# Batch 1's q loaded ahead of two weight tiles, and the last two o quarters of chunk 0 with jt outermost, in an attention and Swish-FFN kernel

## The chip, the core and the metric

The kernel runs on one core of a Trainium2 chip. The metric is device time in microseconds, from one launch to its end. A program's instructions run on five engines, each with its own queue: TensorE (PE, with its weight loads shown apart as PEld), VectorE (DVE), ScalarE (ACT), GpSimd (POOL) and SyncE (SP), which here only issues DMAs. Instructions of one engine run in the order of the program; between engines, semaphores order them.

## What is computed

Eight batches of 8 heads, 576 positions (S), 64 features (D). First a linear attention with a cosine weighting, then a feed-forward layer whose gate is a sigmoid with its own beta per feature:

```python
c, s = cos(pi/2 * pos / S), sin(pi/2 * pos / S)
phi(x) = concat([relu(x) * c, relu(x) * s])      # 64 -> 128 features
kv  = phi(k).T @ v ;  z = sum(phi(k))            # per batch and head
num = phi(q) @ kv  ;  den = phi(q) @ z + 1e-6
x   = (num / den)                                # 4608 tokens x 512
h   = x @ w_in                                   # 512 -> 2048
g   = h * sigmoid(beta * h)
out = g @ w_out                                  # 2048 -> 512
```

Inputs and output are float32; the matmuls run in bf16 with float32 sums.

## The kernel before

**Tiling.** The 4608 tokens are cut into 9 chunks (c) of 512. A chunk has 32 slots. Slots 0 to 15 are `h_group` (L376): for each of 16 blocks of 128 hidden features (jt), four matmuls of 128x512 (`h_mm`, L366) and one Silu on ACT (`h_act`, L373), which makes the tile g. Slots 16 to 31 are the second layer, `o_mm` (L387): four token tiles (tt) of 128 rows, each the sum over the 16 jt, cut into four parts of four jt. In chunk 0 the order is part outermost: slots 16 to 27 walk tt within a part (`o_part`), and slots 28 to 31 each do two tt and two jt (L593). When a tile's last jt is done, ACT copies the sum out (L399) and POOL issues two stores (L386).

**Attention in between.** 64 tokens of one batch's eight heads come from 9 groups (n). For a batch: `q_relu` and `k_relu` (DVE, L190), `v_scale` (DVE L215 and ACT L213), `kv_mm` (PE, L260, 72 small matmuls), `kv_take` out of PSUM (ACT L270 or DVE L272), a turn (transpose) of q, `num_mm` (PE, L281), the division `x_rden` and `x_mul` (DVE, L292 to L303) and a turn of the result into xt, which h_mm reads. From batch 2 on the turns are DMA transposes, and `att_units` puts the batch's work between the slots of the chunk before. For batches 0 and 1 the turns run on PE: `q_turn_pe` (L222), whose two parts are copied out by its `take` (ACT to qt, L235; DVE times tan to qs, L218), and `x_turn_pe` (L335). Chunk 1's tokens are the last group of batch 0 and seven groups of batch 1, so batch 1 has to be ready at the end of chunk 0.

**What sets the order.** The schedule is written by hand: the order of the calls is the order on each engine. The dictionary `early` (L537) says what is done after which slot of chunk 0. Batch 1's sums (`kv_mm`) come after slot 22, its two turns of q after 25 and 26, `num_seven` after 28 and 29, the turns of xs inside slots 30 and 31, around a part of chunk 1's first h matmuls.

**PSUM** is one tile of 8 banks, which the code hands out by number: `h_bank` (L357) for h, and for o of chunk 0 banks 2, 3, 0, 1 for tt 0 to 3.

**Weights and loads.** w_in and w_out come in as float32, four tiles each, through four stage buffers, and are cast to bf16: w_in by DVE and POOL (`cast_win`, L98), w_out by DVE or ACT with a factor 1/beta (`cast_wout`, L110). A stage of w_out can only be loaded when the casts of the w_in tile in the same buffer are done. The loads are issued by SP, in the order of `rest()` (L510): w_out 0 and 1, batch 1's v and k, w_out 2, batch 1's q, w_out 3; batch 2's q, v, k come after slot 24. raw_q, raw_v and raw_k have two buffers each.

**Warm-up matmuls.** `warm_pe` (L418) multiplies zeros, to keep PE busy in the first 20 us: among others 4 of 128 columns (L448), 2 of 512 (L476) and 1 of 512 ahead of the first h matmul (L495).

Of the kernel before, what the change touches and what calls it, by code (L numbers as in the profile page):

```python
# [12 lines left out]
AF = mybir.ActivationFunctionType  # L13
ALU = mybir.AluOpType
# [3 lines left out]
NQ = 9  # L18
# [4 lines left out]
def kernel(  # L23
# [14 lines left out]
    nc = tc.nc  # L38
# [49 lines left out]
    def load_w(kind, i, step=4):  # L88
        if (kind, i) not in stages:
            stages[kind, i] = stage.tile([P, 4, 512], FP32, name="w_stage", tag="w_stage")  # L90
        st = stages[kind, i]
        if kind == "out":
            nc.sync.dma_start(out=st, in_=w_out_v[:, 4 * i : 4 * i + 4, :])
            return
        for a in range(0, 4, step):
            nc.sync.dma_start(out=st[:, a : a + step], in_=w_in_v[:, a : a + step, i * 512 : (i + 1) * 512])

    def cast_win(i, gj, eng="dve", f0=0, f1=512, jps=slice(0, 2)):  # L98
# [8 lines left out]
        else:  # L107
            nc.vector.tensor_copy(o, a)  # L108

    def cast_wout(i, engs="dddd"):  # L110
        st = stages["out", i]
        for jj in range(4):
            j = 4 * i + jj
            if engs[jj] == "a":
                nc.scalar.activation(wout[i][:, jj, :], st[:, jj, :], AF.Copy, scale=rbeta[:, j : j + 1])
            else:
                nc.vector.tensor_scalar(wout[i][:, jj, :], st[:, jj, :],
                                        scalar1=rbeta[:, j : j + 1], scalar2=None, op0=ALU.mult)

    GJ = [(0, 0), (0, 1), (1, 0), (1, 1)]  # L120

# [70 lines left out]
    def q_relu(b, jp, eng="dve"):  # L192
        relu(qb[:, jp].rearrange("q n (j d) -> q j n d", j=2), raw_tile(b, "q")[:, 2 * jp : 2 * jp + 2], eng)
# [28 lines left out]
    def q_turn_pe(b, jp, bank, hold=False):  # L222

        parts = ((0, 0, 5), (1, 5, NQ))
        v2 = []
        for i, n0, n1 in parts:
            t = ps[:, bank + i].bitcast(BF16)[:, 0 : (n1 - n0) * P].rearrange("q (n c) -> q n c", c=P)
            v2.append(t)
            for n in range(n0, n1):
                nc.tensor.matmul(t[:, n - n0, :], lhsT=qb[:, jp, n, :], rhs=ident,  # L230
                                 is_transpose=True, start=(n == n0), stop=(n == n1 - 1))
        def take(e, i):
            _, n0, n1 = parts[i]
            if e == "act":
                nc.scalar.copy(qt[:, jp, n0:n1], v2[i])  # L235
            else:
                tan_mul(nc.vector, qs[:, jp, n0:n1], v2[i], n0, n1)

        if hold:
            return take  # L240
        for e, i in (("act", 0), ("dve", 1), ("act", 1), ("dve", 0)):
            take(e, i)
# [11 lines left out]
    def kv_mm(b, jp, bank, jjs=(0, 1)):  # L254
        t = kv_out(jp, bank)
        for n in range(NQ):
            for jj in jjs:
                for g in range(2):
                    hs = slice(g * HP, (g + 1) * HP)
                    nc.tensor.matmul(  # L260
                        t[jj * HP : (jj + 1) * HP, g], lhsT=rk[hs, n, 2 * jp + jj, :],
                        rhs=vb[hs, n, 2 * jp + jj].rearrange("q s e -> q (s e)"),
                        start=(n == 0), stop=(n == NQ - 1))

    def kv_take(jps, bank, eng="dve"):
        a0, a1 = jps[0], jps[-1] + 1
        o = kv[:, :, a0:a1].rearrange("q g s c e -> q g (s c e)")
        a = ps[:, bank : bank + 2, a0 * 2 * E : a1 * 2 * E]
        if eng == "act":
            nc.scalar.copy(o, a)  # L270
        else:
            nc.vector.tensor_copy(o, a)  # L272
# [83 lines left out]

    def h_bank(c, jt):  # L357
        if c < 2 and jt < 4:
            return ((3, 2, 0, 1), (6, 7, 2, 3))[c][jt]
        return ((6, 7, 4, 5) if c == 0 else (4, 5, 0, 1))[jt % 4]  # L360

    def h_mm(c, jt, mis=range(4), blocks=slice(0, NB)):
        xt = xt_tile(c)
# [7 lines left out]
    def h_act(c, jt):  # L371
        g_t = gt_pool.tile([P, TCH], BF16, name="g_t", tag="g_t")
        nc.scalar.activation(g_t, ps[:, h_bank(c, jt)], AF.Silu, scale=beta[:, jt : jt + 1])  # L373
        gs[c, jt] = g_t
# [10 lines left out]
            eng = (nc.sync, nc.scalar)[hf] if two else nc.sync if c >= 7 else nc.gpsimd  # L385
            eng.dma_start(out=out_v[bb, n][:, m0:m1], in_=o_sb[hf * HP : (hf + 1) * HP, m0:m1])  # L386

    def o_mm(c, tt, jts, between=None):
        o_ps = ps[:, (2, 3, 0, 1)[tt] if c == 0 else 2 + tt % 2]
        for jt in jts:  # L390
            nc.tensor.matmul(o_ps, lhsT=gs[c, jt][:, tt * P : (tt + 1) * P],  # L391
                             rhs=wout[jt // 4][:, jt % 4, :],
                             start=(jt == 0), stop=(jt == JT - 1))
        if jts[-1] < JT - 1:
            return
        if between:
            between()
        o_sb = osb_pool.tile([P, DM], FP32, name="o_sb", tag="o_sb")
        nc.scalar.copy(o_sb, o_ps)  # L399
        store(c, tt, o_sb)  # L400
# [17 lines left out]
    def warm_pe(count, w=512, bank=1):  # L418
        for i in range(count):
            nc.tensor.matmul(ps[:, bank, 0:w], lhsT=zeros[:, 0:P], rhs=zeros[:, 0:w], start=True, stop=True)  # L420
# [24 lines left out]
    warm_pe(8, 128, bank=0 + 2)  # L445
    q_turn_pe(0, 0, 4)
    nc.vector.reciprocal(rbeta, beta)
    warm_pe(4, 128)  # L448
    take = q_turn_pe(0, 1, 2, hold=True)
    warm_long(4)  # L450
    take("act", 0)
# [21 lines left out]
    got = x_rden(2, 0, 0, 7, (0,))  # L473
    got2 = x_rden(4, 0, 7, 8, (0,))
    k_relu(0, 3, 4, "dve", 0, 5)
    warm_pe(2, bank=1)  # L476
    kv_mm(0, 1, 6)
    x_mul_act(got2, 7)
    kv_take((1,), 6, eng="act")
# [12 lines left out]
    x_mul(got, 0, 4)  # L492
    x_mul(got, 4, 7)
    x_mul(x_rden(6, 0, 7, 8, (1,)), 7, 8)
    warm_pe(1, bank=3)  # L495
    h_mm(0, 0, (0, 1))
    h_mm(0, 1, (0, 1))
    x_turn_pe(0, 0, 4, 4, ("act",), (1,))
# [11 lines left out]
    def rest():  # L510

        cast_halves(2, (0,))
        x_mul(x_rden(2, 0, 8, NQ, (0, 1)), 8, NQ)
        cast_halves(2, (256,))
        cast_halves(3)
        load_w("out", 0)
        load_w("out", 1)
        load_raw(1, "v")
        load_raw(1, "k")
        load_w("out", 2)  # L520
        load_raw(1, "q")
        load_w("out", 3)
        cast_wout(0)
        cast_wout(1)
        v_scale(1, 0)
        k_relu(1)
        cast_wout(2)
        q_relu(1, 0)


    def num_seven(jp, bank):
        for n in range(7):
            num_mm(n, jp, bank, n)

    takes = []
    turns = (("act", 0), ("dve", 1), ("act", 1), ("dve", 0))
    early = {  # L537
        4: lambda: (num_mm(8, 0, 2, 0), num_mm(8, 1, 2, 1), rest()),
        9: lambda: x_turn_pe(0, 8, 9, 3),
        15: lambda: v_scale(1, 1, eng="act"),  # L540
        22: lambda: (kv_mm(1, 0, 6), kv_mm(1, 1, 6), kv_take((0, 1), 6, "act"), q_relu(1, 1)),
        25: lambda: takes.append(q_turn_pe(1, 0, 4, hold=True)),
        26: lambda: (takes.append(q_turn_pe(1, 1, 6, hold=True)),
                     [takes[0](*t) for t in turns], cast_wout(3, "adda"),
                     [takes[1](*t) for t in turns]),
        28: lambda: (num_seven(0, 4), x_mul(x_rden(4, 0, 0, 7, (0,)), 0, 7)),
        29: lambda: (num_seven(1, 6), x_mul(x_rden(6, 0, 0, 7, (1,)), 0, 7)),
        31: lambda: ([h_mm(1, jt, (0, 1)) for jt in range(2)], x_turn_pe(1, 0, 7, 5, ("dve",), (1,)),
                     [h_mm(1, jt, (0, 1)) for jt in range(2, 4)]),
    }  # L550

    def num_rest():
        for n in range(7, NQ):
            for jp in range(2):
                num_mm(n, jp, 0, 2 * (n - 7) + jp)
        x_mul(x_rden(0, 0, 7, NQ, (0, 1)), 7, NQ)
        x_turn_dma(1, 7, NQ)

    def att_units(b):
# [21 lines left out]
    for slot in range(32):  # L581
        if slot < 4:
            if slot == 0:
                for jt in range(4):
                    h_mm(0, jt, (2, 3), slice(0, 4))
            h_mm(0, slot, (2, 3), slice(4, 8))
            h_act(0, slot)
        elif slot < 16:
            h_group(0, slot)
        elif slot < 28:  # L590
            o_part(0, slot % 4, (slot - 16) // 4)
        else:
            for tt in (2 * (slot % 2), 2 * (slot % 2) + 1):  # L593
                o_mm(0, tt, range(12, 14) if slot < 30 else range(14, 16),
                     (lambda: x_turn_pe(1, 0, 7, 4, ("act",), (0,))) if tt == 0 else None)
        if slot == 24:
            for name in "qvk":
                load_raw(2, name)
        if slot in early:
            early[slot]()  # L600
    for c in range(1, NTC):
        units = att_units(c + 1) if c + 1 < B else []
        for slot in range(32):
            if c == 1 and slot < 4:
                h_mm(c, slot, (2, 3))
                h_act(c, slot)
            elif slot < 16:
                h_group(c, slot)
            elif c == NTC - 1 and slot >= 28:
                if slot == 28:  # L610
                    o_last(c, 3)
            else:
                o_part(c, (slot - 16) // 4, slot % 4)
            while units and units[0][0] <= slot:
                units.pop(0)[1]()
# [30 lines left out]
```

## Time and profile before

| | |
|---|---|
| median of 4 runs | 295.53 us (295.15 to 296.5) |
| the profiled execution's own time | 296.5 us |
| its span, from first to last instruction | 294.7 us |
| granted TensorE clock, mean | 0.994 |
| PE busy | 287.0 us, 97% of the span |
| HBM read / written | 36.71 MB / 9.44 MB |

The profile is of one execution, the slowest of the four. Times in it count from the start of the span; the 1.8 us between span and time lie outside it. Rows of a timeline give the start, the length and the engine, the line in the code, the operation, what is written and read, and how many instructions were merged; in brackets how long the engine stood idle before, and what ended that. A PE row's length goes to the modelled end of its last matmul, so rows overlap: the distance between the starts of two rows is what the first took. An issue on SP lasts as long as the queue keeps it waiting for space; the time at which the data lands is in the DMA view.

### The profile page before, as it was taken

Reading aid. Unit: us, or ns where it says so; the run is one execution under the profiler, and the core shown is the slowest. Engines: PE = TensorE matmul, PEld = TensorE weight load, DVE = VectorE, ACT = ScalarE, POOL = GpSimd, SP = SyncE. Lnnn points to the kernel's source line nnn. Section 1 sums busy time; section 2 is a strip of 40 time slices with the busy share of each in tenths; the row PEclk is TensorE's granted clock in tenths of the full one; section 3 lists DMA queues with packets and bytes.
Section 4 is the critical chain, followed back from the end, with each engine's and each line's share of the span. In section 5 each row is a group of like instructions: output and inputs, shape, how many; then the busy total and the mean of one; then the engine's idle time right before and its main releaser. Section 6 shows DMA issues by size and latency. Waiting matters only on the chain.

```text
span 294.7 us, 7239 instructions
## 1 busy us (share of the span) xinstructions
PE 287.0 (97%) x3080; PEld 145.7 (49%) x3080; DVE 117.1 (40%) x296; ACT 139.8 (47%) x223; POOL 74.4 (25%) x85
## 2 busy tenths in 40 slices
PE   8789999999999999999999999999999999999995
PEld 7555455455445534455445544554455444444444
DVE  5899978572920293009500870078005000000000
ACT  5558835863157214741375127612761178127611
POOL 1440000632382046402550156014701210000000
PEclk9979999999999999999999999999999999999999
DMA  7999999798999099905992499229201810131033
GB/s 230 384 389 357 392 391 387 208 251 331 166 255 361 6 113 259 400 18 105 208 372 107 97 217 374 101 62 189 55 2 30 160 38 0 38 71 36 0 73 72
DMA packets 50416, 53.82 MB, mean 183 GB/s; under 512 B 30912, under 2 KB 31312, under 8 KB 50384
## 3 DMA queue, kind: packets, MB, share of 16 engines
q1 hardware_dynamic: 47424, 45.88, 51.6%
q0 software_dynamic: 2688, 7.34, 10.8%
q8 instruction: 24, 0.39, 0.5%
q10 hardware_dynamic: 272, 0.14, 0.2%
q14 instruction: 8, 0.07, 0.1%
HBM read 36.71 MB, written 9.44 MB: 157 GB/s over the span
## 4 chain that ended last, share of the span: by engine, by line
PE 93%; DMA 3%; SPq 1%; issue 1%; DVE 0%
PE ps L366 43%; PE ps L391 41%; PE ps L281 4%; DMA raw_v<-in_v_dram 3%; PE ps L260 3%; PE ps L411 1%; SPq L78 1%; PE ps L340 1%; PE ps L230 0%; PE ps L420 0%; DVE rden L296 0%; DVE rk L190 0%; DVE o_sb L414 0%; DVE den L292 0%; DVE vb L205 0%
## 5 line engine op out<-in xcount | busy, mean ns | idle before, releaser
L366 PE MATMUL ps<-xt,win 128*128 128x512 bf16 (+1 forms) x584 | 128.1, 377 | 0.0
L391 PE MATMUL ps<-wout,g_t 128*128 128x512 bf16 x560 | 124.6, 379 | 0.6 <-issue 0.6
L373 ACT ACTIVATE g_t<-ps,beta 128x512 bf16<-128x512 f32 x144 | 98.2, 688 | 33.1 <-PE ps L366 33.1
L366 PEld LDWEIGHTS <-win 128*128 128x128 bf16 x584 | 56.4, 98 | 65.4 <-issue 0.7
L391 PEld LDWEIGHTS <-g_t 128*128 128x128 bf16 x560 | 54.0, 98 | 64.4 <-issue 0.9
L386 POOL DMA_DIRECT2D out_dram<-o_sb x56 | 38.0, 683 | 145.1 <-ACT o_sb L399 145.1
L399 ACT COPY o_sb<-ps 128x512 f32<-128x512 f32 x35 | 20.2, 589 | 97.5 <-PE ps L391 97.5
L272 DVE CAST kv<-ps 128x520 bf16<-128x520 f32 x6 | 4.2, 700 | 67.8 <-PE ps L260 67.8
L218 POOL TENSOR_TENSOR qs<-qt,tanr 128x1152 bf16<-128x1152 bf16 x12 | 28.6, 2405 | 6.3 <-DVE vb L215 6.2
L414 DVE COPY o_sb<-ps 128x256 f32<-128x256 f32 (+1 forms) x2 | 0.7, 358 | 62.9 <-PE ps L411 62.9
L303 DVE TENSOR_TENSOR xs<-ps,rden 128x768 bf16<-128x768 f32 (+5 forms) x27 | 23.1, 863 | 0.8
L215 DVE TENSOR_SCALAR vb<-raw_v,cos 128x256 bf16<-128x256 f32 x63 | 17.1, 348 | 0.0
L292 DVE TENSOR_TENSOR den<-ps,eps 128x12 f32<-128x12 f32 (+4 forms) x26 | 4.2, 160 | 32.2 <-PE ps L281 32.2
L215 DVE TENSOR_SCALAR vb<-raw_v,sin 128x256 bf16<-128x256 f32 x54 | 14.7, 353 | 0.0
L281 PEld LDWEIGHTS <-qt 64*64 64x64 bf16 x576 | 10.8, 108 | 4.8 <-issue 4.4
L260 PE MATMUL ps<-vb,rk 64*64 64x130 bf16 x576 | 10.3, 219 | 2.4 <-ACT rk L188 2.2
L108 DVE CAST win<-w_stage 64x512 bf16<-64x512 f32 x27 | 12.0, 443 | 0.6
L281 PE MATMUL ps<-kv,qt 64*64 64x65 bf16 x576 | 12.0, 197 | 0.2 <-ACT kv L270 0.2
L190 DVE TENSOR_SCALAR qb<-raw_q 128x1152 bf16<-128x1152 f32 x16 | 11.4, 752 | 1.4 <-DMA raw_q<-in_q_dram 1.3
L281 PE MATMUL ps<-kv,qs 64*64 64x65 bf16 x576 | 11.8, 196 | 0.0
L260 PEld LDWEIGHTS <-rk 64*64 64x64 bf16 x576 | 8.6, 107 | 6.4 <-ACT rk L188 3.1
L190 DVE TENSOR_SCALAR rk<-raw_k 128x2304 bf16<-128x2304 f32 (+2 forms) x9 | 10.8, 1201 | 0.0
(58 smaller groups left out, 101.5 us busy)
## 6 DMA issues: line engine op xcount, KB each, us to landing
raw_v<-in_v_dram SPq DMA_DIRECT2D x7, 1152.0 KB, 11.2
raw_k<-in_k_dram SPq DMA_DIRECT2D x7, 1152.0 KB, 13.6
raw_q<-in_q_dram SPq DMA_DIRECT2D x7, 1152.0 KB, 7.4
out_dram<-o_sb POOLq DMA_DIRECT2D x56, 128.0 KB, 3.9
w_stage<-in_moe_w_out_dram SPq DMA_DIRECT2D x4, 1024.0 KB, 9.7
w_stage<-in_moe_w_in_dram SPq DMA_DIRECT2D x3, 1024.0 KB, 14.0
out_dram<-o_sb SPq DMA_DIRECT2D x14, 128.0 KB, 2.4
raw_q<-in_q_dram SPq DMA_DIRECT2D x2, 576.0 KB, 4.5
```

The costliest lines, as they stand in the source:

```text
L108: nc.vector.tensor_copy(o, a)
L190: nc.vector.tensor_scalar(dst, src, scalar1=0.0, scalar2=None, op0=ALU.max)
L215: nc.vector.tensor_scalar(o, a, scalar1=t[:, n : n + 1], scalar2=None, op0=ALU.mult)
L218: eng.tensor_tensor(dst.rearrange("q n (g p) -> q n g p", g=2), src.rearrange("q n (g p) -> q n g p", g=2), tanr[:, n0:n1].unsqueeze(2).to ...
L260: nc.tensor.matmul(t[jj * HP : (jj + 1) * HP, g], lhsT=rk[hs, n, 2 * jp + jj, :], rhs=vb[hs, n, 2 * jp + jj].rearrange("q s e -> q (s e)") ...
L281: nc.tensor.matmul(ps[cols, bank + jj, slot * E : (slot + 1) * E], lhsT=(qt, qs)[cs][rows, jp, n, cols], rhs=kv[rows, g, jp, cs, :], start ...
L303: nc.vector.tensor_tensor(o.rearrange("q j n s d -> q j (n s) d"), nv[:, :, a:z, :, 0:D].rearrange("q j n s d -> q j (n s) d"), rden[:, :, ...
L366: nc.tensor.matmul(ps[:, h_bank(c, jt), blocks.start * 64 : blocks.stop * 64], lhsT=win[jt // 4][:, mi, (jt % 4) * P : (jt % 4 + 1) * P], ...
L373: nc.scalar.activation(g_t, ps[:, h_bank(c, jt)], AF.Silu, scale=beta[:, jt : jt + 1])
L386: eng.dma_start(out=out_v[bb, n][:, m0:m1], in_=o_sb[hf * HP : (hf + 1) * HP, m0:m1])
L391: nc.tensor.matmul(o_ps, lhsT=gs[c, jt][:, tt * P : (tt + 1) * P], rhs=wout[jt // 4][:, jt % 4, :], start=(jt == 0), stop=(jt == JT - 1))
L399: nc.scalar.copy(o_sb, o_ps)
```

## The change

- Batch 1's q is issued right behind its k, ahead of w_out 2 and 3, and these two are loaded in halves of 512 KB.
- `cast_wout` becomes `cast_out`, for one jt at a time. The casts of w_out 2 and 3 (j = 8 to 15) are taken out of `rest()` and put among the takes of the turned q (`second`), some on DVE, some on ACT. Both `q_relu` of batch 1 stand at the end of `rest()`.
- In chunk 0, slots 24 to 31 are one jt each, for all four tt. Batch 1's sums and its first turn of q come after slot 22, the second after 23, `num_seven` after 24 and 26, the two turns of xs after 28 and 29.
- Chunk 1's h matmuls are no longer begun in chunk 0: its slots 0 to 3 are whole groups. `h_bank` and the banks of `num_rest` follow from that.
- Of the warm-ups, 4 of 128 columns become 1 of 512, 2 of 512 become 1, and the one ahead of the first h matmul goes.

```diff
@@ load_w
-        if kind == "out":
-            nc.sync.dma_start(out=st, in_=w_out_v[:, 4 * i : 4 * i + 4, :])
-            return
         for a in range(0, 4, step):
+            if kind == "out":
+                nc.sync.dma_start(out=st[:, a : a + step], in_=w_out_v[:, 4 * i + a : 4 * i + a + step, :])
+                continue
@@ casts of w_out
-    def cast_wout(i, engs="dddd"):
+    def cast_out(j, eng="d"):
+        i, jj = divmod(j, 4)
...
@@ h_bank
-            return ((3, 2, 0, 1), (6, 7, 2, 3))[c][jt]
-        return ((6, 7, 4, 5) if c == 0 else (4, 5, 0, 1))[jt % 4]
+            return ((3, 2, 0, 1), (6, 7, 4, 5))[c][jt]
+        return ((6, 7, 4, 5) if c == 0 else (0, 1, 4, 5))[jt % 4]
@@ warm-ups
-    warm_pe(4, 128)
+    warm_pe(1)
...
-    warm_pe(2, bank=1)
+    warm_pe(1, bank=1)
...
-    warm_pe(1, bank=3)
@@ rest
-        load_w("out", 2)
         load_raw(1, "q")
-        load_w("out", 3)
-        cast_wout(0)
-        cast_wout(1)
+        load_w("out", 2, 2)
+        load_w("out", 3, 2)
+        for j in range(8):
+            cast_out(j)
         v_scale(1, 0)
         k_relu(1)
-        cast_wout(2)
         q_relu(1, 0)
+        q_relu(1, 1)
@@ early
+    def second():
+
+        takes.append(q_turn_pe(1, 1, 6, hold=True))
+        cast_out(8)
+        takes[0]("act", 0)
+        takes[0]("dve", 1)
+        cast_out(9, "a")
+        takes[0]("dve", 0)
+        takes[0]("act", 1)
+        cast_out(10)
+        for e, i in (("act", 0), ("dve", 1), ("act", 1), ("dve", 0)):
+            takes[1](e, i)
+        cast_out(11, "a")
+        cast_out(12)
+        for j in range(13, JT):
+            cast_out(j, "a")
...
-        22: lambda: (kv_mm(1, 0, 6), kv_mm(1, 1, 6), kv_take((0, 1), 6, "act"), q_relu(1, 1)),
-        25: lambda: takes.append(q_turn_pe(1, 0, 4, hold=True)),
-        26: lambda: (takes.append(q_turn_pe(1, 1, 6, hold=True)),
-                     [takes[0](*t) for t in turns], cast_wout(3, "adda"),
-                     [takes[1](*t) for t in turns]),
-        28: lambda: (num_seven(0, 4), x_mul(x_rden(4, 0, 0, 7, (0,)), 0, 7)),
-        29: lambda: (num_seven(1, 6), x_mul(x_rden(6, 0, 0, 7, (1,)), 0, 7)),
-        31: lambda: ([h_mm(1, jt, (0, 1)) for jt in range(2)], x_turn_pe(1, 0, 7, 5, ("dve",), (1,)),
-                     [h_mm(1, jt, (0, 1)) for jt in range(2, 4)]),
+        22: lambda: (kv_mm(1, 0, 6), kv_mm(1, 1, 6), kv_take((0, 1), 6, "act"),
+                     takes.append(q_turn_pe(1, 0, 4, hold=True))),
+        23: second,
+        24: lambda: (num_seven(0, 4), x_mul(x_rden(4, 0, 0, 7, (0,)), 0, 7)),
+        26: lambda: (num_seven(1, 6), x_mul(x_rden(6, 0, 0, 7, (1,)), 0, 7)),
+        28: lambda: x_turn_pe(1, 0, 7, 4, ("act",), (0,)),
+        29: lambda: x_turn_pe(1, 0, 7, 5, ("dve",), (1,)),
@@ num_rest: bank 0 becomes bank 2
@@ chunk 0
-        elif slot < 28:
+        elif slot < 24:
             o_part(0, slot % 4, (slot - 16) // 4)
         else:
-            for tt in (2 * (slot % 2), 2 * (slot % 2) + 1):
-                o_mm(0, tt, range(12, 14) if slot < 30 else range(14, 16),
-                     (lambda: x_turn_pe(1, 0, 7, 4, ("act",), (0,))) if tt == 0 else None)
+            for tt in range(4):
+                o_mm(0, tt, (slot - 16,))
@@ chunks 1 to 8
-            if c == 1 and slot < 4:
-                h_mm(c, slot, (2, 3))
-                h_act(c, slot)
-            elif slot < 16:
+            if slot < 16:
                 h_group(c, slot)
```

## The prediction, made before the changed kernel had run

> **What bounds the kernel now.** I read the page's totals and its chain first, then the lists of waits, then the timelines of the two stretches that the change touches.
>
> ```profile
> PE 287.0 (97%) x3080; PEld 145.7 (49%) x3080; DVE 117.1 (40%) x296; ACT 139.8 (47%) x223; POOL 74.4 (25%) x85
> PE 93%; DMA 3%; SPq 1%; issue 1%; DVE 0%
> ```
>
> The chain that ended last is TensorE for 93%. The list of waits gives PE 4.2 us of waiting in all, and none of it between 16 and 104 us. So a reordered stage can save no wait; it can only save PE instructions, or add waits. PE's timeline before the dense part, and the clock there (columns of the second view: span, then busy us of PE, PEld, DVE, ACT, POOL, then granted clock, DMA share, GB/s):
>
> ```profile
> 13.15 0.61 PE L420 MATMUL ps<-zeros 128*128 128x512 bf16 x2
> 15.45 0.24 PE L260 MATMUL ps<-vb,rk 64*64 64x130 bf16 x2 [1.69 <-ACT rk L188]
> 18.68 0.61 PE L420 MATMUL ps<-zeros 128*128 128x512 bf16 x1
> 19.09 1.36 PE L366 MATMUL ps<-xt,win 128*128 128x512 bf16 x4
> ```
> ```profile
> 16.30:19.70 3.40, 3.40 (x97) 2.38 (x86) 3.24 (x8) 1.45 (x3) 3.05 (x5) 0.51 1.06 391
> ```
>
> After the 1.69 us gap the clock is granted at half for 3.4 us. The zero matmul at 18.68 (L495) lies in that half-clock stretch and delays the first h matmul to 19.09: 0.41 us. From 13.54 to 32.3 VectorE is nearly never idle (takes of num, then the casts of w_in), and h_mm uses each cast soon after it ends:
>
> ```profile
> 27.00 5.28 DVE L108 CAST win<-w_stage 64x512 bf16<-64x512 f32 x12
> 32.31 3.26 DVE L117 TENSOR_SCALAR wout<-w_stage,rbeta 128x512 bf16<-128x512 f32 x8
> ```
>
> The last cast of w_in 3 ends at 32.28. The second matmul of slot 14 needs it; its weight load ran at 32.45 and the matmul at 32.66.
>
> The stage that is reordered (PE, ACT and DVE rows of one timeline):
>
> ```profile
> 40.31 1.22 PE L260 MATMUL ps<-vb,rk 64*64 64x130 bf16 x72
> 41.45 2.76 PE L391 MATMUL ps<-wout,g_t 128*128 128x512 bf16 x12
> 44.05 0.67 PE L230 MATMUL ps<-ident,qb 128*128 128x128 bf16 x9
> 41.97 0.59 ACT L270 CAST kv<-ps 128x520 bf16<-128x520 f32 x1 [3.32 <-PE ps L260]
> 39.78 1.68 DVE L117 TENSOR_SCALAR wout<-w_stage,rbeta 128x512 bf16<-128x512 f32 x4 [0.58 <-DMA w_stage<-in_moe_w_out_dram]
> 42.78 1.43 DVE L190 TENSOR_SCALAR qb<-raw_q 128x1152 bf16<-128x1152 f32 x2 [1.32 <-DMA raw_q<-in_q_dram]
> ```
>
> DVE waits here for w_out 2, then for q, but PE has o matmuls to do meanwhile and doesn't wait. SP's issues for it:
>
> ```profile
> 25.43 1.40 SPq L78 DMA_DIRECT2D raw_k<-in_k_dram  x1
> 28.76 0.37 SPq L93 DMA_DIRECT2D w_stage<-in_moe_w_out_dram  x1
> 29.17 1.59 SPq L78 DMA_DIRECT2D raw_q<-in_q_dram  x1
> 32.31 1.40 SPq L93 DMA_DIRECT2D w_stage<-in_moe_w_out_dram  x1
> ```
>
> With the DMA view's time to landing (11.6, 11.0, 13.6, 13.1 us) these landed at 37.0, 39.8, 42.8 and 45.4. The queue is full: 3.0 us for each raw tensor, 2.7 for each w_out.
>
> **The change, part by part.**
>
> *Warm-ups.* (1) Four 128-wide zero matmuls become one 512-wide: the same 512 columns (0.42 us, 6.87 to 7.29), so 0. (2) One of two at 13.15 goes. What follows waits for rk until 15.45 anyway: 0, except that the gap grows from 1.69 to 1.9 us, and with it the chance of a cold clock. (3) The one at 18.68 goes. Four half-clock h matmuls then start 0.41 earlier, but the clock comes back at the same 19.75, so only one matmul of full-clock time, 0.216, is won. What is late next: x_turn needs xs, which DVE ends at 19.96 (0.16 to 0.2 can pass); slots 10, 12 and 14 need the casts. Slot 14 allows most narrowly: cast end 32.28, plus 0.06 (rk ended at 15.86, its matmul ran at 15.92), plus a weight load of 0.10, is 32.44 against 32.66: 0.22. So -0.2; bounds 0 (DVE gates after all) and -0.41.
>
> On this the Trainium skill ("TensorE: Matmul & The Clock Gate", section "Why this matters for your kernels") asks for no idle gap over about 3 us. Here a gap of 1.69 us was followed by 3.4 us at half clock, so the trace is stricter than the rule. By the rule the sum has 0 for (2) for certain; by the trace it has 0 with C's risk below.
>
> *DMA order.* SP stands idle from 26.83 to 28.76 for the w_in 2 casts (L93's buffer is theirs). q's buffer is free, so q goes right behind k. In a full queue bytes land in order: q at 37.0 + 3.0 = 40.0 (was 42.8), w_out 2's halves at 41.4 and 42.8 (was 39.8), w_out 3's at 44.1 and 45.4. What follows (batch 2's q, v, k, issued from 33.75) finds the same bytes ahead of it: unchanged at 48.4, 51.5, 54.6. Each half adds one issue of 0.37 us on a queue that is blocked by space anyway: 0. In the stretch 13.5 to 15.5, when 288 and 512 KB transfers were moved, the view shows 403 GB/s, no less than with 1 MB ones (367 to 393 from 24 to 46 us).
>
> The skill's "DMA: Bandwidth & Descriptors", section "Bandwidth", advises at least 1 MiB for a DMA, and its section "Anatomy of one DMA" fits a fixed 2.0 us to each (on the software path; these go by the hardware one). As an estimate from that page the two added DMAs would bring w_out 3's end up to 4 us later; the row of 403 GB/s speaks against it.
>
> *Matmul order.* The same 64 o matmuls, 72 kv, 18 turns of q, 112 num and 14 turns of xs in the stage. jt outermost changes the bank at every matmul; dense matmuls issue 0.216 apart whether the bank changes or not at the group borders that the trace has. 0, bounds 0 and 0.3 (32 matmuls of slots 24 to 31 at 0.01 each; the groups of 12 and 4 that follow a turn or kv show no more than that beyond 0.216). The switch from dense to 64x64 matmuls costs about 0.1 (28 took 6.14, not 6.04); before and after have it for kv, num, num and num_rest: 0. Batch 1's turn of xs no longer stands between chunk 1's h matmuls, and its rows (0.40 and 0.39) are the same: 0.
>
> *New waits on PE.* In before's clock, PE after the change: kv 40.31 to 41.45; turn 1 41.45 to 41.95; slot 23 to 42.81; turn 2 to 43.31; slot 24 to 44.17; num.
> Turn 1 needs q_relu: DVE's k_relu ends at 39.2, q lands at 40.0, 0.75: 40.8. Cover 0.6 us. Behind it on DVE stands q_relu(1,1), to 41.5, then the cast of j = 8 (0.48), then qs: a late w_out 2 holds these up, and num with them.
> num needs both takes. ACT, in program order: kv at 41.97, then, each less 0.09 overlap (7 of 0.69 took 4.29), qt 42.5, cast 9 (1.33 for two) 43.1, qt to 44.3. DVE: cast 8 to 41.9, turn 1 done 42.1, qs to 42.8, qs (needs ACT's first copy, 43.1) to 44.0. PE would be at num at 44.17, 44.28 with the switch; ACT is done at 44.3 + 0.06. +0.1, bounds 0 and +1.4: w_out 2's first half may come until 42.4 without cost; if it takes 13.1 us, like w_out 3's, from its issue at 30.6 (q's issue blocked until 29.5), it lands at 43.7.
> num 2 at 46.7 needs turn 2's takes (ACT 45.5, DVE 45.9) and slots 25 to 29 need casts 9 to 13 (43.8, 44.4, 46.1, 46.2, 46.7) at 45.0, 45.8, 47.4, 48.2, 49.5: covered by 0.8 us and more. x_mul ends at 47.8 and 49.3, the turns of xs come at 49.1 and 50.4, their copies end at 50.5 and 51.5, chunk 1 starts at 52.5: covered. The four copies of o end at 54.1, the first g of chunk 1 follows; slot 6 is the first to need one of its banks, at 58: covered by 2 us. num_rest (banks 2, 3) needs the first two copies, 53.1, at 53.4: covered by 0.3.
> The new bank orders of chunks 1 to 8 have DVE's x_mul out of banks 0 and 1 twelve slots (over 10 us) ahead of their use: 0.
>
> **Sum**, against the profiled execution (span 294.7, its time 296.5): -0.2 + 0 + 0 + 0.1 = -0.1, so span 294.6. That execution was the slowest of four; its median is 295.53. The same -0.1 on the median: **295.4 us**, no change.
>
> **Rivals.**
> A, *more is won*: PE is nowhere late, the whole 0.41 comes through: 295.1, and with small losses at group borders gone, 294.6. For: the takes' wait is only 0.06 by my sum. Against: the casts allow 0.22.
> B, *slower: w_out 2 arrives behind q too late for cast 8*, which now stands ahead of the takes on DVE and ACT. Place: num in slot 24. It decides from a landing at 42.4, 1:1. At 43.7: +1.3 to 1.4, 296.8. For: DVE waited for just this tile at 39.78 with everything in front of q; landings spread over 2 us between DMA engines. Against: 1.0 us of cover over the byte count.
> C, *slower: cold clock*. The longer gap makes the throttle last a second 3.4 us: half of it, 1.7, less 0.2 slack: 296.9. For: the gap threshold isn't known. Against: PE is busy from 15.9 on without a break, as before.
> D, *the load doesn't move*: q lands at 42.8 as before, turn 1 waits until 43.6 instead of 41.45: +2.1, 297.6. Against: the issue has no wait of its own, and SP stood idle.
>
> **How the numbers follow.** About 0.5% (1.5 us) is what a measurement of this kernel can tell from no change. Forecast (295.0 to 295.9) 0.62; A 0.16; B 0.12, half of it over 297.0; C 0.06, a third over; D 0.03, all over 297.0; unforeseen 0.01. Slower: 0.06 + 0.02 + 0.03 = 0.11; faster (under 294.05): 0.03 out of A's tail and the unforeseen; same: 0.86. The range takes A's 294.6 and B's 296.8.
>
> **What would show it.** Right: first h matmul near 18.7, slot 4 about 0.2 earlier; DVE's q_relu near 40.1; cast 8 near 41.5 without a DMA wait over 0.3; PE waiting under 0.2 before L281 near 44.3; chunk 1 from 52.2 to 52.6. Wrong: a PE gap before L230 or L281, a DVE wait for w_stage past 42.4, a second clock slice under 0.9 after 20 us, o matmuls over 0.22 us apart in slots 24 to 31.

## The result, and the profile after

| | before | after |
|---|---|---|
| median | 295.63 us (76 runs, 294.81 to 296.88) | 295.97 us (53 runs, 294.39 to 298.57) |
| ratio | | 1.0021, interval 1.0011 to 1.0032 |
| profiled execution: time, span, clock | 296.5, 294.7, 0.994 | 295.65, 293.9, 1.0 |

The kernel became slower by 0.2%: little, but the interval leaves out 1. I had forecast 0.1 us less. 295.97 lies inside the range of 294.6 to 296.8 and just outside the 295.0 to 295.9 that had a chance of 0.62. The new thing is the spread: the slowest run of after is 1.7 us above the slowest of before. Each run lists its mean granted clock, and sorted by it the runs of after fall into three groups:

| mean clock of the run | runs of after | their times, median | runs of before beside the experiments | their median |
|---|---|---|---|---|
| 0.997 to 1.0 | 18 | 294.39 to 295.95, 295.20 | 87 | 295.36 |
| 0.992 to 0.994 | 21 | 295.34 to 297.07, 296.06 | 17 | 296.02 |
| 0.987 to 0.988 | 15 | 297.08 to 298.57, 297.51 | 0 | |

One stretch of 3.4 us at half clock takes 1.7/294 = 0.006 off the mean, so the groups are none, one and two such stretches. Group by group after is not slower than before; it has more runs with a stretch, 36 of 54 against 17 of 104. The runs of before in the table are from the other sets, since the 76 above have no clock on record. Without the 15 runs of the last group the median of after is 295.64, against 295.63 of before; leaving out the slowest runs lowers any median, so this alone proves nothing. The profiled execution, with clock 1.0, is not one of them; it tells nothing of the last group, but it answers the other steps. The page's totals, and the chain that ended last:

```profile
PE 285.6 (97%) x3075; PEld 144.3 (49%) x3075; DVE 115.5 (39%) x293; ACT 141.8 (48%) x226; POOL 74.8 (25%) x85
PE 85%; DMA 8%; DVE 3%; SPq 2%; issue 1%
```

PE's share of the chain fell from 93% to 85%: the chain now runs over q's load. PE's timeline of after, the start and the reordered stage:

```profile
13.77 0.24 PE L259 MATMUL ps<-vb,rk 64*64 64x130 bf16 x2 [0.72 <-ACT rk L187]
16.38 1.24 PE L365 MATMUL ps<-xt,win 128*128 128x512 bf16 x4
18.54 0.40 PE L339 MATMUL ps<-ident,xs 128*128 128x128 bf16 x4 [0.93 <-DVE xs L302]
...
38.80 1.22 PE L259 MATMUL ps<-vb,rk 64*64 64x130 bf16 x72
40.68 0.68 PE L229 MATMUL ps<-ident,qb 128*128 128x128 bf16 x9 [0.66 <-DVE qb L189]
41.19 1.03 PE L390 MATMUL ps<-wout,g_t 128*128 128x512 bf16 x4
```

The gap ahead of the second sums is 0.72 us here, not 1.69, and no half-clock stretch follows; the first h matmul starts at 16.38, but DVE's xs holds the next step 0.93 us. Further on PE waits 0.66 us ahead of batch 1's first turn, where I had counted 0.6 us of cover. What it waits for, DVE's row and SP's issues:

```profile
39.86 1.43 DVE L189 TENSOR_SCALAR qb<-raw_q 128x1152 bf16<-128x1152 f32 x2 [1.65 <-DMA raw_q<-in_q_dram]
```
```profile
23.96 0.51 SPq L78 DMA_DIRECT2D raw_k<-in_k_dram  x1
24.51 0.85 SPq L78 DMA_DIRECT2D raw_q<-in_q_dram  x1
27.29 7.62 SPq L94 DMA_DIRECT2D w_stage<-in_moe_w_out_dram  x4
```

q is issued right behind k and landed at 39.86; I had predicted 40.0. The load moved as the change says. PE came to the place 1.5 us sooner than in the profile of before (kv at 38.80, not 40.31), and so the load was late for it.

### The profile page after: what moved, and what is told of

It reads as the page before. It is cut to its first block, busy times and chain, and to the rows that moved or that the text cites. A ratio compares the mean times of both kernels' runs of the same rounds, so it can differ in the third digit from the quotient of the medians.

```text
span 293.9 us, 7219 instructions
## 1 busy us (share of the span) xinstructions
PE 285.6 (97%) x3075; PEld 144.3 (49%) x3075; DVE 115.5 (39%) x293; ACT 141.8 (48%) x226; POOL 74.8 (25%) x85
## 4 chain that ended last, share of the span: by engine, by line
PE 85%; DMA 8%; DVE 3%; SPq 2%; issue 1%
PE ps L390 39%; PE ps L365 38%; DMA raw_q<-in_q_dram 5%; PE ps L280 3%; DMA raw_k<-in_k_dram 3%; PE ps L259 2%; DVE win L108 2%; SPq L78 2%; PE ps L408 1%; DVE xs L302 1%; PE ps L229 0%; PE ps L339 0%; DVE qb L189 0%; DVE rk L189 0%; DVE rden L295 0%
## 5 line engine op out<-in xcount | busy, mean ns | idle before, releaser
L385 POOL DMA_DIRECT2D out_dram<-o_sb x56 | 38.7, 695 | 142.4 <-ACT o_sb L396 142.4
L189 DVE TENSOR_SCALAR qb<-raw_q 128x1152 bf16<-128x1152 f32 x16 | 11.4, 752 | 1.7 <-DMA raw_q<-in_q_dram 1.7
```

Source lines behind the costliest of these rows:

```text
L189: nc.vector.tensor_scalar(dst, src, scalar1=0.0, scalar2=None, op0=ALU.max)
```

## The experiments

Three theories. **T1**: the removed zero matmuls left gaps, and the gaps the cold clock. **T2**: the new order of the stage costs, and the zero matmuls are free. **T3**, formed after the first four runs: PE's instructions arrive in blocks, and with fewer instructions ahead of a certain place the next block is asked for too late. Line numbers of rows are those of each kernel.

**1. The changed kernel with all three warm-ups as before.**
```diff
-    warm_pe(1)
+    warm_pe(4, 128)
-    warm_pe(1, bank=1)
+    warm_pe(2, bank=1)
+    warm_pe(1, bank=3)
```


> The changed kernel with the three zero-matmul edits undone (4 of 128 columns, 2 of 512 at the gap ahead of batch 0's second kv sums, 1 of 512 ahead of the first h matmul); the order and the loads stay changed. Theory T1 (the fewer zero matmuls let the clock fall to half for one or two stretches of 3.4 us, each costing 1 to 2 us, and the new order is neutral or better): no run with a mean granted clock under 0.99, median 295.0 to 295.5, ratio to before 0.997 to 1.000. Theory T2 (the new order costs, by the wait of the turn of q for batch 1's q, 0.7 us in the profile, and the zero matmuls are free): median 295.9 to 296.3 and runs up to 298 as in the changed kernel.

Measured: 296.56 us, ratio 1.0031 (1.0017 to 1.0045). No run of 12 at 0.988: the third group is gone, as T1 says, but the median is no better, so something else costs as well, as T2 says.

**2. The kernel before with the changed warm-ups alone.**
```diff
-    warm_pe(4, 128)
+    warm_pe(1)
-    warm_pe(2, bank=1)
+    warm_pe(1, bank=1)
-    warm_pe(1, bank=3)
```


> The kernel before with the three zero-matmul edits alone. T1: runs split by the granted clock as in the changed kernel, a quarter of them at 0.987 to 0.988 and over 297, median 296 to 297, slower than before. T2: as before, 295.2 to 295.6, or 0.2 faster.

Measured: 297.04 us, ratio 1.0043 (1.0024 to 1.0062); 5 of 12 runs at 0.988, none at 1.0. The warm-up edit alone makes the third group.

**3 and 4. The changed kernel with one warm-up back**, the second matmul in the gap, or the one ahead of the first h.
```diff
# 3
-    warm_pe(1, bank=1)
+    warm_pe(2, bank=1)
# 4
+    warm_pe(1, bank=3)
```


> The changed kernel with the second zero matmul in the gap ahead of batch 0's second kv sums put back, the other two edits kept. T1, if the gap is what lowers the clock: like the kernel with all three back, median 295.0 to 295.5, no clock under 0.99. T1, if it is the zero matmul ahead of the first h matmul: still a quarter of the runs at 0.988, median near 296. T2: 295.9 to 296.3 in any case.

> The changed kernel with the one zero matmul ahead of the first h matmul put back, the other two edits kept. T1, if this one is what lowers the clock (it stands ahead of a wait of 0.9 us of the turn of xs in the changed kernel's profile): median 295.0 to 295.5, no clock under 0.99. T1, if it is the gap: a quarter of the runs at 0.988 still. T2: 296.1 to 296.5, since it adds 0.2.

Measured: 297.28 us, ratio 1.0057 (1.0035 to 1.0078), and 298.86 us, ratio 1.0102 (1.0076 to 1.0128). With the gap filled one run of six was in the third group and the median was no better; with a warm-up behind the gap five of six were there (0.986 to 0.989: the longer the span, the less two stretches take off its mean). Both speak against T1. The profile of the second, PE's timeline, shows the execution that after's profile had missed:

```profile
13.96 0.58 PE L259 MATMUL ps<-vb,rk 64*64 64x130 bf16 x17 [1.04 <-ACT rk L187]
17.58 0.75 PE L259 MATMUL ps<-vb,rk 64*64 64x130 bf16 x19 [3.04 <-issue]
```

PE stops 3.04 us in the middle of the second kv sums, after 17 of 36 matmuls, and "issue" says that it waited for no data and no engine. The windows of the same kernel (span, busy us of PE, PEld, DVE, ACT, POOL, granted clock, DMA share, GB/s):

```profile
16.00:23.00 7.00, 5.09 (x100) 3.57 (x102) 3.33 (x11) 1.45 (x3) 2.13 (x4) 0.51 1.05 386
```

Half clock for about 7 us: two of the stretches. The DMA view has a queue q8 of kind "instruction": 24 packets, 0.39 MB, in the whole run. PE has 6,160 matmuls and weight loads on the page of before; 0.39 MB over these is about 64 B each, and 24 x 256 = 6,144. I read this as the queue that brings PE's instructions, 16 KB or about 256 at a time. The DMA view of the kernel before, from 9.5 to 12.5 us, and of kernel 4, from 14 to 16.5 us (packets, MB, share):

```profile
q1 hardware_dynamic: 560, 1.16, 102.2%
q8 instruction: 1, 0.02, 2.1%
```
```profile
q1 hardware_dynamic: 487, 0.96, 102.0%
q8 instruction: 1, 0.02, 2.8%
```

In before a block's transfer starts at 10.34, well ahead of its use. In kernel 4 none runs between 8 and 14 us; one runs from 15.03 to 16.15, and PE goes on at 17.58. Kernel 2's PE stops the same way: 2.48 us, behind the 17th matmul, block from 14.19 to 15.24, on again at 16.82. That gave T3: 4 matmuls of 128 columns made into 1 are 6 instructions fewer (3 matmuls, 3 weight loads) ahead of q's second turn. I took it that the place where the next block is asked for thereby moves from among these warm-ups to behind the start of that turn. The trace doesn't show the asking: 256 instructions counted back from the stop end inside that turn in before's order as in after's, so the place is a guess.

**5. The changed kernel with as many instructions ahead, and as little work.** Four more zero matmuls at the very start, in as many columns.
```diff
-    warm_pe(58, 48)
+    warm_pe(62, 45)
```


> The changed kernel with the 58 zero matmuls of 48 columns at the start made 62 of 45 columns: as much PE time (2784 and 2790 columns), but 8 more instructions ahead of batch 0's second kv sums, as many as the kernel before had there. Theory T3 (PE's instructions arrive in blocks by DMA; with 8 fewer instructions the border of a block lies where the next block comes late, PE stops inside the second kv sums, at its 17th matmul, for 2.5 to 3 us, and the clock falls for two stretches): no such stop, no run at 0.988, median 295.2 to 295.6, ratio to before 0.998 to 1.000. Theory T1 (it is the missing PE work that lowers the clock): a quarter of the runs at 0.988 and over 297, median near 296, as in the changed kernel.

Measured: 296.02 us, ratio 1.0016 (1.0004 to 1.0028); none of 8 runs at 0.988. The block's transfer starts at 9.90, and PE doesn't stop:

```profile
14.51 1.15 PE L259 MATMUL ps<-vb,rk 64*64 64x130 bf16 x34 [0.22 <-DVE rk L189]
```

**6. The kernel before with fewer instructions ahead**, the columns about the same.
```diff
-    warm_pe(58, 48)
+    warm_pe(54, 52)
```


> The kernel before with the 58 zero matmuls of 48 columns made 54 of 52: as much PE time (2808 columns), but 8 fewer instructions ahead of the second kv sums, as in the changed kernel. T3: the stop of 2.5 to 3 us inside the second kv sums in some runs, with mean clocks of 0.988 and times over 297, median 296 to 297. T1: as before, 295.4 to 295.8, no clock under 0.99.

Measured: 297.65 us, ratio 1.0059 (1.0034 to 1.0084), 5 of 10 runs at 0.988, with nothing of the change in it. With experiment 5 this settles it: the number of instructions makes the third group, not the work or the gaps. (None of 8 alone could be luck, where 15 of 54 are the rule; 8, 10 and 13, which have the added instructions too, bring it to none of 43.) The two runs at full clock took 294.61 and 295.07, quicker than most of before; the first of these, profiled, had no stop, with its block at 11.13.

**7. Experiment 5, with q behind w_out 2 again.**
```diff
-        load_raw(1, "q")
         load_w("out", 2, 2)
+        load_raw(1, "q")
```


> The changed kernel with the shifted rows, and batch 1's q loaded behind w_out 2 again (w_out in halves). The matmul order stays. Both theories: q lands at 42.8, the first turn of q waits for it. If q's load is what the new matmul order needs, PE's wait there is 2.1 to 3.6 us and the median 297.0 to 298.5; if it does not matter, the same as with the shifted rows alone.

Measured: 298.76 us, ratio 1.0125 (1.0105 to 1.0144), 2.7 us above experiment 5. PE's timeline shows the price:

```profile
43.02 0.68 PE L229 MATMUL ps<-ident,qb 128*128 128x128 bf16 x9 [2.58 <-DVE qb L189]
```

One of its four runs was at 0.989 although the block's place was before's. I have no profile of that run. In the profiled one the wait of 2.58 us brought no half clock: its only stretch, from 7.64 to 11.06, lies among the warm-ups. So what cooled that run is open.

**8. Experiment 5, with the turns and num one slot later.**
```diff
-        22: lambda: (..., takes.append(q_turn_pe(1, 0, 4, hold=True))),
-        23: second,
-        24, 26: num_seven and x_mul;  28, 29: x_turn_pe
+        23: lambda: (takes.append(q_turn_pe(1, 0, 4, hold=True)), second()),
+        25, 27: num_seven and x_mul;  29, 30: x_turn_pe
```


> The changed kernel with the shifted rows, and the first turn of q behind slot 23 (ahead of the second turn), num behind slots 25 and 27, the turns of xs behind 29 and 30. If the wait of the first turn for q (0.66 us in the profile of the changed kernel) is a loss: 0.3 to 0.7 faster than with the shifted rows alone, 294.6 to 295.2, and no gap on PE ahead of the turn. If it only hides another wait (the takes ahead of num): no gain, the gap stands ahead of num.

Measured: 295.79 us, ratio 1.0015 (1.0002 to 1.0028). PE's wait for q, 0.21 us in experiment 5, is gone. Against experiment 5's 1.0016 that can't be told apart, so the wait isn't shown to be what was left.

**9 and 10. Borders moved to better places.** Before and after, each with as many instructions ahead of the asking place as before, and 8 fewer behind it (chunk 0's jt 3 has its last sums in one piece); 10 with experiment 8's order too.
```diff
# both
-                for jt in range(4):
+                for jt in range(3):
-            h_mm(0, slot, (2, 3), slice(4, 8))
+            h_mm(0, slot, (2, 3), slice(4 if slot < 3 else 0, 8))
# 9, on before:  warm_pe(2, bank=1) -> warm_pe(1, bank=1);  warm_pe(1, bank=3) taken out
# 10, on after:  warm_pe(58, 48) -> warm_pe(61, 46)
```


> The kernel before, with 8 instructions fewer behind the place where the load of PE's second block is asked for: one of the two zero matmuls of 512 columns in the gap, the one ahead of the first h matmul, and one h block of chunk 0 whose last two sums are done in one piece instead of two halves of 256 columns. All that stands ahead of that place is as before. T3 (the load of the block is late only if the place where it is asked for moves behind the wait for q): no stop in the second kv sums, no run at 0.988; the stop of 0.6 us near 104 us goes, as in all kernels with 8 or 10 fewer instructions: 294.7 to 295.2, faster than before by 0.4 to 0.9. If it is the total of instructions ahead of the kv sums, or the zero matmuls' time, that matters: runs at 0.988 and over 297.

> The changed kernel with 61 zero matmuls of 46 columns at the start (6 instructions more, as many as were taken ahead of the place where the block is asked for), the one h block in one piece, and the turns of q behind slot 23. T3: no run at 0.988, no stop near 104 us, PE waits for neither q nor the takes by more than 0.2: 294.5 to 295.2, as fast as the kernel before with the same instructions taken out, or 0.2 faster. T1: as the changed kernel.

Measured: **294.75 us, ratio 0.9973 (0.9961 to 0.9985)** for 9, the fastest kernel of the study, quicker than both; 295.45 us, ratio 1.0000 (0.9988 to 1.0013) for 10, slower than I expected. No run of either at 0.988. These two are the best measure of the new order, loads and banks by themselves: one set of runs, as many weight loads on PE (3,076), no third group, and 10 takes 0.70 us longer.

**11. The load order alone**, on the kernel before: q ahead of w_out 2 and 3, these in halves (the diff of `load_w` and `rest` above, without the casts).

> The kernel before with the order of the loads alone: batch 1's q ahead of w_out 2 and 3, these in halves. w_out 2 lands 2 to 3 us later, and the old matmul order needs it before q: its third jt is cast at 43.2, and slot 24 reaches it between 41.2 and 42.8, so PE waits 0.4 to 2.0 us there: 296.0 to 297.5. If the order of the loads does not matter by itself: 295.4 to 295.8.

Measured: 296.59 us, ratio 1.0036 (1.0025 to 1.0048). PE waits for the casts of w_out 2:

```profile
41.66 0.77 PE L391 MATMUL ps<-wout,g_t 128*128 128x512 bf16 x2 [0.71 <-DVE wout L117]
43.03 1.64 PE L391 MATMUL ps<-wout,g_t 128*128 128x512 bf16 x6 [0.60 <-DVE wout L117]
```

So neither half stands alone: the old matmul order wants w_out 2 first (11), the new one q (7).

**12. The changed kernel with 6 instructions more behind the asking place.**
```diff
-    warm_pe(1, bank=1)
+    warm_pe(4, 128, bank=1)
```


> The changed kernel with the zero matmul of 512 columns ahead of the second kv sums in four of 128: the same PE time, 6 instructions more behind the place where the block is asked for, none ahead of it; the border of the block moves from the 17th to the 14th matmul of the second kv sums. If the place of the border decides: no run at 0.988, 295.2 to 296.0. If the place of asking decides: a quarter or more of the runs at 0.988 and over 297, as in the changed kernel.

Measured: 296.86 us, ratio 1.004 (1.0012 to 1.0069), 4 of 12 runs at 0.986 to 0.988. PE's timeline:

```profile
13.93 0.57 PE L259 MATMUL ps<-vb,rk 64*64 64x130 bf16 x14 [0.71 <-ACT rk L187]
17.14 0.86 PE L259 MATMUL ps<-vb,rk 64*64 64x130 bf16 x22 [2.65 <-issue]
```

The stop moved from the 17th to the 14th matmul: 3 matmuls are 6 instructions, as T3 counts. In 2, 4 and 12 PE has done exactly 222 weight loads when it stops, which is what a border at a fixed count would make. The border's place in the sums doesn't cure it. 10 and 12 both add 6 instructions to after, 10 at the start and 12 in the gap: none of 12 runs against 4 of 12. So it is the count ahead of some earlier place that matters, as T3 has it.

**13 and 14. The bank order of h in chunks 2 to 8**: put back in experiment 10, and made new in experiment 9.
```diff
# 13
-        return (... (0, 1, 4, 5))[jt % 4]
+        return (... (0, 1, 4, 5) if c == 1 else (4, 5, 0, 1))[jt % 4]
# 14
-        return (... (4, 5, 0, 1))[jt % 4]
+        return (... (4, 5, 0, 1) if c == 1 else (0, 1, 4, 5))[jt % 4]
```


> The changed kernel as in e10 (rows shifted, one h block in one piece, turns of q behind slot 23), with the bank order of h of the kernel before (4, 5, 0, 1) in chunks 2 to 8. If the new bank order of the later chunks brings the stop of 0.5 to 0.7 us near 193 us, which the profiles of the kernels with the changed order have: 0.4 to 0.6 faster than e10, the stop gone, 294.7 to 295.0. If the stop comes from elsewhere (where the block's load is asked for in chunk 0): 295.2 to 295.6, the stop stays.

> The kernel before as in e9 (8 instructions fewer behind the place of asking), with the changed kernel's bank order of h (0, 1, 4, 5) in chunks 2 to 8 and nothing else of the change. If the bank order brings the stop near 193 us: 0.4 to 0.6 slower than e9, 295.1 to 295.5. If not: as e9, 294.6 to 294.9.

Measured: 295.07 us, ratio 0.9987 (0.9974 to 1.0000), against 1.0000 for 10; and 295.40 us, ratio 0.9996 (0.9983 to 1.0010), against 0.9973 for 9. Both point the same way, the new order costing 0.4 to 0.7 us, but each pair was run in two sets, and the intervals overlap (for 9 and 14 by 0.0002). Where it may go: a stop by "issue" behind the last num of a batch near 193 us. PE's timelines of 9 and 14, then of 10 and 13:

```profile
192.77 4.48 PE L391 MATMUL ps<-wout,g_t 128*128 128x512 bf16 x20 [0.23 <-issue]
```
```profile
193.39 3.83 PE L391 MATMUL ps<-wout,g_t 128*128 128x512 bf16 x17 [0.45 <-issue]
```
```profile
192.93 4.26 PE L390 MATMUL ps<-wout,g_t 128*128 128x512 bf16 x19 [0.66 <-issue]
```
```profile
192.65 4.70 PE L390 MATMUL ps<-wout,g_t 128*128 128x512 bf16 x21 [0.16 <-issue]
```

It grows from 0.23 to 0.45, and shrinks from 0.66 to 0.16 from 10 to 13. It too looks like a late block: in 10 one is transferred from 190.26 to 191.33 and PE goes on at 192.93; in 13 the transfer starts 0.48 us earlier, at 189.78. The kernels of a pair have the same number of PE instructions, so the place of the borders is the same; why the banks move the block's time stays open. And the pair of 9 and 14 is weaker than it looks. Where chunk 2 begins, before any changed bank is used, the profiled run of 14 is already 0.40 us behind that of 9 (82.73 and 82.33), for it had waited for a cast of w_out 3, whose load was late:

```profile
46.27 1.02 PE L391 MATMUL ps<-wout,g_t 128*128 128x512 bf16 x4 [0.66 <-ACT wout L115]
```

So only 0.22 of the 0.64 us between these two executions is the stop.

## Why the prediction was wrong

**The warm-ups, step (1): this is the step that failed.** I had costed "four 128-wide zero matmuls become one 512-wide" by their columns: "the same 512 columns, so 0". The columns are the same; the instructions are 6 fewer, and that was the price. Where the block is late, PE stops 2.5 to 3.0 us, and the clock falls to half for two stretches. In the six kernels with 6 to 8 fewer instructions ahead (after, 2, 3, 4, 6, 12), 35 of 100 runs were at 0.986 to 0.989. In the nine others with the old number or more (before, 1, 5, 8, 9, 10, 11, 13, 14) none of 191 was, and in 7 one of 4. That the count decides is shown by 5 and 6 and by the 222 weight loads; that it acts through the place of asking is inferred, from 10 against 12 and from the start of the block's transfer in the profiles (9.8 to 10.3 us in kernels with the old count or more, 10.9 to 15.0 with fewer). For after itself it is read from its runs' clocks; its own profile has no late block.

**Rival C** had the outcome, a second cold stretch, 296.9 us, and gave it 0.06. The third group has 297.51 and is 15 of 54 runs. Its cause was wrong: I had the gap's length, and with the gap's matmul back (3) the loss was still there: median 297.28. A median over 53 runs shows only 0.34 us of it.

**Step (2)** isn't settled. In after's profile the gap is 0.72 us with no cold stretch, but in that of 5 it is 1.03 us, and the clock is at half from 14.58 to 18.00. After also has more runs with one stretch than before, 21 of 54 against 17 of 104; experiment 3, with the gap's matmul back, had four of six, so the shorter warm-up isn't shown to make them.

**Step (3)** was sized on a profile with a cold stretch. At full clock DVE gates the start, with the matmul or without: PE waits 0.93 us for xs in after, and as long in experiment 6, which still has it:

```profile
18.86 0.40 PE L340 MATMUL ps<-ident,xs 128*128 128x128 bf16 x4 [0.93 <-DVE xs L303]
```

So in such runs (3) is worth 0, the bound that I gave for this case, and not -0.2.

**The load of q** was right in place (40.0 predicted, 39.86 measured) and wrong in what PE would do: "cover 0.6 us" became a wait of 0.66. I had taken PE's times from one execution, the slowest of four, with a cold stretch. In after PE reached this place 1.5 us sooner, but the loads gained little: k, ahead of q in the queue, was issued 1.5 us sooner and was there at 36.85 instead of 37.0. Rival D's price for a load that doesn't move, +2.1, is 2.7 us in experiment 7, and the wait 2.58.

**w_out 2, rival B**, never decided. Cast 8 starts at 41.22 without a wait; num wasn't late. The halves show no cost: 389 GB/s from 24 to 46 us.

**The matmul order** with jt outermost was 0, as predicted: the eight o matmuls that start at 44.09 are followed by num at 45.92, and 1.83 us is 8 of 0.216 and the 0.1 of the switch.

**The new bank orders** I had at 0, by DVE's cover of ten us. The medians say 0.4 to 0.7 us, the stops near 193 us 0.2 to 0.5, neither for certain, and why the banks should move a block I don't know. With the loads, the matmul order and 8's shift they are what 10 has more than 9: 0.70 us, where my sum had 0.1. This is the second place where the sum was wrong.

**Sum.** Two causes share the loss, and their parts in the median aren't settled. Taking the third group out brings after's median to before's, but keeping the block in time doesn't: experiment 5 still stands at 1.0016 (1.0004 to 1.0028), and its six runs at full clock have a median of 296.02, against 295.20 for after's 18. Its 8 added instructions move every later border, and its wait for q is only 0.21 us; what the rest is I haven't found. That the two kernels are so close at full clock is partly luck: before has a stop of 0.62 us near 104 us that after hasn't, and after has one of 0.56 near 193.

On this the Trainium skill bears with "Runtime: NRT & Kernel Launch", section "Instruction fetch mechanics". It says that an engine's instructions are refilled in blocks of 16 KiB, 256 instructions, by a DMA queue of the sequencer, and that the cost of crossing a block is mostly hidden. The size agrees with this trace: 24 packets for 6,160 matmuls and weight loads. The cost does not: PE stood 2.48 to 3.04 us at one border.

## What to carry to other kernels

Count PE instructions as well as columns when warm-ups or splits are changed: a few more or fewer move every later border between instruction blocks, and a late block cost 2.48 to 3.04 us here, where the work taken out was to save 0.2. Look at the clock of all runs, not at the median and one profile: the execution that was profiled may be one of the good ones. When cover is counted against a load, take PE's times from a full-speed execution: here a cold stretch held PE back by 1.5 us and k's landing by 0.15.

## What the runs showed of the hardware

- A stop of PE marked "issue" can be the arrival of its instructions. PE went on 1.4 to 1.6 us after the block's last byte (16.15 to 17.58 in experiment 4, 15.24 to 16.82 in 2). Two smaller stops have the same look: before's of 0.62 us near 104 us, with a block at 102.08 to 103.39 and on again at 104.69, and after's of 0.56 near 193, with a block at 191.12 to 192.08 and on again at 193.52.
- While the data queue moved 380 to 406 GB/s, the block of kernels with fewer instructions ahead started its transfer either at 10.9 to 11.4 us or at 14.2 to 15.0 us, never between in six profiles. Why it is sometimes 4 us later is open; the moment of asking isn't in the trace.
- The half clock came in stretches of 3.4 us or two of these. In experiments 2, 4 and 12 it began inside the stop of 2.5 to 3.0 us and lasted 6.8 us (16.20 to 23.03 in 4). The length of a gap alone doesn't decide: 1.69 us (before) and 1.03 us (5) were followed by 3.4 us at half clock, 1.60 us in the same place (1) and the wait of 2.58 us ahead of 43.02 us (7) by none.
